# Attention feeding a channel mix: mu spread by one fp32 matmul, wk loaded by whole rows, one load on another queue, new planner settings

## The chip, the cores and the metric

The kernel runs on one core of one Trainium2 chip. The metric is device time in microseconds (us). An execution's profile gives a span from the first to the last instruction; the device time of the same execution is a little longer.

## The reference

```python
q_s = exp(q - max_d(q));  q_s /= sum_d(q_s)        # q, k, v: (8 batches, 8 heads, 576, 64)
k_s = exp(k - max_s(k));  k_s /= sum_s(k_s)
attn = q_s @ (k_s^T @ v)                           # per batch and head
x = attn, heads side by side                       # (8, 576, 512)
x_prev = x shifted by one position, zero first
xk = mu_k * x + (1 - mu_k) * x_prev                # mu_k, mu_r: 512 values
xr = mu_r * x + (1 - mu_r) * x_prev
k = relu(xk @ w_k);  v = (k * k) @ w_v             # w_k 512x1024, w_v 1024x512
out = sigmoid(xr @ w_r) * v                        # w_r 512x512, fp32 out
```

The kernel drops the maxima, since exp of these inputs is small, and works its matmuls in bf16.

## The kernel before

**Tiling.** A batch is done as two groups g = 0, 1 of four heads. Positions are laid as 64 partitions by J = 9, two heads on one partition column block, so that a raw tile (`raw_a` to `raw_l`, twelve buffers) holds q, k or v of one batch and group in fp32: two halves `u`, 288 KB each. Channels of the channel mix are four tiles `ct` of 128; group g makes tiles 2g and 2g+1. F is eight tiles `fc`.

**Attention of one group.** ScalarE: exp of q (`eq`) and k (`ek`), cast of v (`vv`). VectorE: row sums and reciprocals of q (`rsum`, `rrec`, L427 and L430), scaled q (`qs`, L435). TensorE: nine transposes (L462), whose result ScalarE copies to `qt` (L466); the k-v product with a column of ones (L443), whose column sums give `rz` (L450, L454). For batch 0 VectorE multiplies the k-v product with `rz` and with `mu_mask` into `wp` (L503), so that TensorE makes the mixed `xk` and `xr` by itself (L515) and ScalarE or VectorE only copies them out (L520). For batches 1 to 7 TensorE makes x (L556) with weights `w` (L550), ScalarE copies it (`xb`, L561), and VectorE does the rest: an edge copy, the difference `xd` (L569), its scaling by `mu` (`xm`, L574) and the sum `xk` or `xr` (L579).

**mu.** `mu` (one column per mu and channel tile) comes from `mu_sb` by a small TensorE transpose (L324) and a VectorE copy (L327). `mu_rows` holds the 512 values of each mu on every partition, loaded by four broadcast DMAs of 64 partitions x 1 KB (L333). GpSimd builds `mu_mask` from it (L340, L341), four operations for each mu, in the blocks that VectorE has cleared (L305).

**The channel mix** runs in units of 512 columns of `xk`/`xr` (256 for every fifth): k parts (L636, TensorE, 32 matmuls of 128x512), relu on ScalarE (L621), square on VectorE (L625); then for each 128 positions an r part (L667, four matmuls), tanh on ScalarE (L672), two v parts (L677, four matmuls each), the gate on VectorE (L683) and the store from SP (L693). The first two units are "early": for four `fc` at a time they do channel tiles 0 and 1, and then 2 and 3, since group 0 of a batch is mixed before group 1.

**Weights.** `wk`, `wr` and `wv` are cast to bf16 by DMAs from GpSimd's queue. `wk` comes in halves h of 512 columns of F, each half as two DMAs of 64 partitions. A manual dependency holds the first of them until a load of batch 0 (`first[GATE]`) has landed. The loads of batch 1 and later follow on the same queue. [...]

**Order.** Everything is handed to a planner, which simulates five engines with the costs given to `plan.add` and picks, on each engine, the operation with the best pair (start, key); `LOOK` says how much later an operation may start and still count as ready, `key` is a due time passed back along the dependencies (`SPARE` is added at each step, `AHEAD` moves the mixing of batch 0, 1 and later ones forward). `DMA_RATE`, `DMA_LEAD` and `DMA_TAIL` say when a load is believed to land. Engines run their lists strictly in the order so found. `mm` is four PSUM banks, `att` two pairs of banks.

Of the kernel before, what the change touches and what calls it, by code (L numbers as in the profile page):

```python
# [8 lines left out]
ACT = mybir.ActivationFunctionType  # L9
# [3 lines left out]
F32 = mybir.dt.float32  # L13
# [3 lines left out]
START = 0.7  # L17
HOP = 0.05
LATE = 1e6
SPARE = 0.0  # L20
LOOK = {"PE": 0.03, "ACT": 0.3, "DVE": 0.2, "POOL": 0.03, "SP": 0.03}
AHEAD = (0.0, 2.0, 5.0)
MAIN = 18.5
PACE = 1.23
DMA_RATE = 395.0
DMA_LEAD = 1.9
DMA_TAIL = 0.6

PARTS = {1: [slice(0, 2)], 2: [slice(0, 1), slice(1, 2)]}
FIRST = ((0, 0, ("SP", "ACT")), (1, 0, ("SP", "ACT")), (0, 1, ("SP", "SP")),  # L30
         (0, 2, ("SP", "SP")), (1, 1, ("SP", "SP")), (1, 2, ("SP", "SP")))
ORDER = (0, 1, 2)
SOON = {(1, 0, 0): 1.2, (1, 0, 1): 1.4, (1, 0, 2): 1.5}
GATE = 7
FILL = 0
ON_PE = (0,)
CASTS = (("ACT", "ACT"), ("ACT", "ACT"))
# [24 lines left out]
class Plan:  # L62
# [57 lines left out]
    def order(self):  # L120
        self.set_due()
        free = {}
        self.pe_busy = []
        dma_free = 0.0
        waiting = {}
        for op in self.ops:
            waiting.setdefault(op.engine, []).append(op)
        done = []
        left = len(self.ops)
        while left:  # L130
            chosen = None
            for engine, ops in waiting.items():
                now = free.get(engine, START)
                ready = None
                for op in ops:
                    if any(d.end is None for d in op.deps):
                        continue
                    t = max([now] + [d.end + HOP for d in op.deps])
                    ok = True
                    for slot in op.takes:  # L140
                        got = self.slot_time(slot)
                        if got is None:
                            ok = False
                            break
                        t = max(t, got[0] + HOP)
                    if not ok:
                        continue
                    rank = (max(t, now + LOOK[engine]), op.key)
                    if ready is None or rank < ready[0]:
                        ready = (rank, t, op)  # L150
                if ready is not None and (chosen is None or ready[1] < chosen[1]):
                    chosen = ready
            assert chosen is not None, "no operation can start"
            _, t, op = chosen
            for slot in op.takes:
                slot.index = self.slot_time(slot)[1]
                for part in self.pools[slot.pool][slot.index]:
                    self.user[part] = slot
            occ, lat = op.occ, op.lat
            if op.engine == "PE" and not self.warm(t):  # L160
                occ, lat = 2 * occ, occ + lat
            op.start, op.end = t, t + lat
            if op.size:
                dma_free = max(dma_free, t + DMA_LEAD) + op.size / DMA_RATE
                op.end = dma_free + DMA_TAIL
            if op.engine == "PE":
                self.pe_busy.append((t, t + occ))
            free[op.engine] = t + occ
            waiting[op.engine].remove(op)
            done.append(op)  # L170
            left -= 1
        return sorted(done, key=lambda o: o.start)
# [3 lines left out]
def kernel(  # L176
# [12 lines left out]
    nc = tc.nc  # L189

    B, H, S, D = q.shape
    C = H * D
    F = moe_w_k.shape[1]
    assert S == 576 and D == 64 and H == 8, f"{q.shape=}"
    J = S // 64
    CT = C // 128
# [9 lines left out]
    plan = Plan(pools, shared)  # L206

    const = ctx.enter_context(tc.tile_pool(name="const", bufs=1))
# [28 lines left out]
    def bank(slot):  # L237
        return ps[slot.pool][slot.index][:]
# [7 lines left out]
    wk_bf = const.tile([128, CT, F], BF16, name="wk_bf")  # L246
    wv_bf = const.tile([128, FT, C], BF16, name="wv_bf")
    wr_bf = const.tile([128, CT, C], BF16, name="wr_bf")
    mu_sb = const.tile([8, 128], F32, name="mu_sb")
    mu = const.tile([128, 8], F32, name="mu")  # L250
    ident = const.tile([128, 128], BF16, name="ident")
    identf = const.tile([8, 8], F32, name="identf")
    mu_rows = const.tile([128, 2, CT, 64], F32, name="mu_rows")
    mu_mask = const.tile([128, 2, 2, CT, 128], F32, name="mu_mask")
    warm = const.tile([1, 1], F32, name="warm")

# [41 lines left out]

    def emit_consts():
        nc.vector.tensor_copy(out=identf[:], in_=ident[0:8, 0:8])  # L300
        for t in vvs:
            nc.vector.memset(t[:, :, 128:130], 1.0)

# [7 lines left out]
            nc.vector.memset(t[:, :, 0:1], 0.0)  # L311

    zero = plan.add("DVE", 0.1, 0.15, -10, emit_warm_zero)
    plan.add("ACT", 2.0, 2.0, 1.5, emit_warm, [zero])
    mu_load = plan.add("POOL", 1.2, 1.2, -9.2, emit_mu_load, size=8.0)
    identity = plan.add("POOL", 0.6, 0.8, -9.1, emit_identity)
    consts = plan.add("DVE", 0.2, 0.3, -9, emit_consts, [identity])
    late_consts = plan.add("DVE", 0.6, 0.7, LATE, emit_late_consts)
    mask_zeros = plan.add("DVE", 1.8, 1.9, 0, emit_mask_zeros)

    mu_slot = Slot("mm")

    def emit_mu():
        nc.tensor.transpose(out=bank(mu_slot)[:, 0:8], in_=mu_sb[:], identity=identf[:])  # L324
# [1 line left out]
    def emit_mu_copy():  # L326
        nc.vector.tensor_copy(out=mu[:], in_=bank(mu_slot)[:, 0:8])  # L327

    def emit_mu_rows_load(m):
        src = (moe_mu_k, moe_mu_r)[m]  # L330
        for u in range(2):
            ap = bass.AP(tensor=src.tensor, offset=src.offset + 256 * u, ap=[[0, 64], [1, 256]])
            nc.gpsimd.dma_start(  # L333
                out=mu_rows[64 * u:64 * u + 64, m, :, :].rearrange("p c e -> p (c e)"), in_=ap)

    def emit_mu_mask(m):

        for u in range(2):
            r = slice(64 * u, 64 * u + 64)
            nc.gpsimd.tensor_copy(out=mu_mask[r, m, 0, :, r], in_=mu_rows[r, m, :, :])  # L340
            nc.gpsimd.tensor_scalar(out=mu_mask[r, m, 1, :, r], in0=mu_rows[r, m, :, :],  # L341
                                    scalar1=-1.0, scalar2=1.0, op0=ALU.mult, op1=ALU.add)

    mu_t = plan.add("PE", 0.2, 0.4, -500, emit_mu, [mu_load, consts], [mu_slot])
    mu_done = plan.add("DVE", 0.08, 0.17, 0, emit_mu_copy, [mu_t], gives=[mu_slot])
    mu_masked = []
    for m in range(2):
        o = plan.add("POOL", 1.4, 1.4, -9.5 + m, lambda m=m: emit_mu_rows_load(m), size=131.0)
        mu_masked.append(plan.add("POOL", 1.6, 1.7, -2 + m, lambda m=m: emit_mu_mask(m),
                                  [o, mask_zeros]))  # L350

    def filler(slot):
        for _ in range(2):
# [6 lines left out]
                 [slot])  # L360

    def weight_part(dst, src, n, u, c0, c1):
        ap = bass.AP(tensor=src.tensor, offset=src.offset + 4 * u * D * n + c0,
                     ap=[[n, 64], [D * n, CT], [1, c1 - c0]])
        return nc.gpsimd.dma_start(out=dst[64 * u:64 * u + 64, :, c0:c1], in_=ap)

    gate = [first[GATE]]
    sync = mybir.DependencyInfo(mybir.DependencyClass.Sync, mybir.DependencyReason.DATA)

    def emit_wk(h):  # L370
        for u in range(2):
            ld = weight_part(wk_bf, moe_w_k, F, u, 512 * h, 512 * h + 512)
            if h == u == 0:
                tc.add_manual_dep(ld.ins, gate[0].made.ins.name, sync)

    wk_done, wv_done = [], []
    for h in range(2):
        wk_done.append(plan.add(
            "POOL", 1.25, 1.25, h, lambda h=h: emit_wk(h), gate, size=1048.0))
    wr_done = plan.add("POOL", 1.25, 1.25, 2, lambda: [  # L380
        weight_part(wr_bf, moe_w_r, C, u, 0, C) for u in range(2)], gate, size=1048.0)

    def emit_wv(h):
        n = FT // 2
# [4 lines left out]
    for h in range(2):  # L389
        wv_done.append(plan.add("POOL", 0.75, 0.75, 3 + h, lambda h=h: emit_wv(h), gate,  # L390
                                size=1048.0))
# [217 lines left out]
    def unit(half, c0, n):  # L609
# [33 lines left out]
        for f0 in range(0, FT, step):  # L643
            kfs = [Slot("mm") for _ in range(step)]
            mms_ = [None] * step
            for cts in ((0, 1), (2, 3)) if early else (range(CT),):
                gs = sorted({ct // 2 for ct in cts})
                for i in range(step):
                    fc = f0 + i
                    mms_[i] = plan.add(  # L650
                        "PE", per * len(cts), per * len(cts) + 0.17, clock,
                        lambda kf=kfs[i], fc=fc, cts=cts: k_part(kf, fc, cts),
                        [o for b in bs for g in gs for o in mixed[b, g, 0]]
                        + [wk_done[fc // 4], mms_[i]],
                        [kfs[i]] if cts[0] == 0 else [])
                    clock += PACE * per * len(cts)
            for i in range(step):
                kdone.append(mms_[i])
                relu_square(f0 + i, kfs[i], mms_[i])
        rdone = []  # L660
        for m in range(n // 128):
            c = c0 + 128 * m
# [24 lines left out]
            def store(ot=ot, c=c, half=half):  # L687
                for i in range(2):
# [7 lines left out]
            r = plan.add("PE", 0.864, 1.03, clock, r_part,  # L696
                         [o for b in own for g in range(2) for o in mixed[b, g, 1]] + [wr_done],
                         [rps])
            rdone.append(r)
            t = plan.add("ACT", 0.476, 0.6, clock + 1.5, tanh, [r], [th], [rps])  # L700
            clock += PACE * 0.864
            o = plan.add("PE", 0.864, 1.03, clock, lambda v=v_part: v(range(0, 4)),
                         squares[0:4] + wv_done[0:1], [vps])
# [4 lines left out]
            o = plan.add("DVE", 0.593, 0.683, clock + 1.5, gated, [o, t], [ot], [vps, th])  # L708
# [51 lines left out]
```

The softmax here doesn't subtract the row's maximum and nothing guards it: scores larger than these inputs give would overflow.

## Time and profile before

| what | us |
|---|---|
| median of 8 runs | 214.12 (213.27 to 215.41) |
| the profiled execution | 214.17 |
| its span | 212.4 |
| TensorE busy | 190.8 |
| VectorE busy | 163.3 |
| ScalarE busy | 151.9 |
| GpSimd busy | 44.8 |

The profile gives each engine's busy time, the chain of waits that ended last, and the instructions in order of time with the idle time before each and what ended it. Busy time is an average over the span; a stretch of it has to be looked at by itself to see which engine or transfer is late there. For DMAs that cast, the bytes that the profile counts are those written.

### The profile page before, as it was taken

What the parts mean: (1) busy time and instruction counts of PE and PEld (TensorE: products, weight loads), DVE (VectorE), ACT (ScalarE), POOL (GpSimd) and SP (SyncE); (2) the same over time, 40 slices, a digit from 0 to 9 for tenths busy, and PEclk for the clock granted to TensorE, in tenths of its full rate; (3) what the DMA queues carried; (4) which work ended last, traced back from release to release, by engine and by line L of the source; (5) the groups of instructions that cost most, each with busy time, mean ns of one, the idle gap of its engine ahead of it and who ended that gap; (6) DMA issues with size and microseconds to landing.
All of it is one profiled execution on the core that took longest, in us unless ns stands there. A gap on an engine that the chain in (4) does not pass through costs nothing.

```text
span 212.4 us, 3596 instructions
## 1 busy us (share of the span) xinstructions
PE 190.8 (90%) x1281; PEld 97.1 (46%) x1281; DVE 163.3 (77%) x363; ACT 151.9 (72%) x228; POOL 44.8 (21%) x76
## 2 busy tenths in 40 slices
PE   0279698977999999999999999999999999999990
PEld 0254244533544445544466544454544554444740
DVE  4947561999999999999988999698779548942521
ACT  4684696999799999697449997956794665452430
POOL 7385744744433422121000000000000000000000
PEclk9999999999999999999999999999999999999999
DMA  6999999999999999889371040422043022402514
GB/s 217 317 253 204 319 203 378 386 409 404 391 401 400 393 412 403 305 233 302 99 221 39 3 99 0 100 57 47 0 99 90 12 52 49 99 0 49 125 28 99
DMA packets 16530, 40.88 MB, mean 192 GB/s; under 512 B 2360, under 2 KB 4928, under 8 KB 16512
## 3 DMA queue, kind: packets, MB, share of 16 engines
q0 software_dynamic: 9024, 27.66, 40.1%
q1 hardware_dynamic: 7200, 12.39, 20.5%
q10 hardware_dynamic: 288, 0.59, 0.8%
q8 instruction: 10, 0.16, 0.3%
q14 instruction: 8, 0.07, 0.1%
HBM read 33.82 MB, written 9.44 MB: 204 GB/s over the span
## 4 chain that ended last, share of the span: by engine, by line
PE 75%; DMA 12%; DVE 7%; ACT 1%; POOL 1%; SPq 1%; issue 1%; DVEq 0%
PE mm_b L677 9%; PE mm_a L677 7%; PE mm_d L677 7%; PE mm_a L636 6%; PE mm_c L636 6%; PE mm_b L636 6%; PE mm_c L677 5%; PE mm_d L667 5%; PE mm_d L636 5%; DMA wv_bf<-in_moe_w_v_dram 4%; DMA wk_bf<-in_moe_w_k_dram 4%; DMA raw_d<-in_v_dram 4%; PE mm_c L667 4%; PE mm_a L667 3%; PE att_b L443 3%; PE att_a L462 2%
## 5 line engine op out<-in xcount | busy, mean ns | idle before, releaser
L636 PEld LDWEIGHTS <-wk_bf 128*128 128x128 bf16 x320 | 30.6, 98 | 36.0 <-issue 6.5
L636 PE MATMUL mm_c<-xk,wk_bf 128*128 128x512 bf16 (+1 forms) x88 | 21.7, 359 | 4.3 <-DVE xk L579 2.2
L677 PEld LDWEIGHTS <-k_a 128*128 128x128 bf16 x144 | 13.3, 98 | 16.2 <-issue 1.4
L636 PE MATMUL mm_a<-xk,wk_bf 128*128 128x512 bf16 (+1 forms) x84 | 20.5, 359 | 0.1
L667 PEld LDWEIGHTS <-xr 128*128 128x128 bf16 x144 | 13.3, 98 | 15.3
L677 PEld LDWEIGHTS <-k_b 128*128 128x128 bf16 x144 | 13.3, 98 | 15.0
L636 PE MATMUL mm_d<-xk,wk_bf 128*128 128x512 bf16 (+1 forms) x72 | 18.0, 361 | 0.0
L636 PE MATMUL mm_b<-xk,wk_bf 128*128 128x512 bf16 (+1 forms) x76 | 17.7, 351 | 0.0
L677 PE MATMUL mm_b<-wv_bf,k_a 128*128 128x512 bf16 x56 | 14.4, 379 | 0.0
L462 PE MATMUL att_a<-ident,qs_a 128*128 128x128 bf16 x72 | 5.8, 231 | 8.2 <-DVE qs_a L435 8.2
L667 PE MATMUL mm_d<-wr_bf,xr 128*128 128x512 bf16 x48 | 12.3, 380 | 0.0
L677 PE MATMUL mm_a<-wv_bf,k_b 128*128 128x512 bf16 x48 | 12.3, 379 | 0.0
L677 PE MATMUL mm_d<-wv_bf,k_a 128*128 128x512 bf16 x40 | 10.3, 379 | 1.1 <-DMA wv_bf<-in_moe_w_v_dram 1.1
L667 PE MATMUL mm_c<-wr_bf,xr 128*128 128x512 bf16 x40 | 10.3, 379 | 0.0
L677 PE MATMUL mm_b<-wv_bf,k_b 128*128 128x512 bf16 x40 | 10.1, 379 | 0.0
L462 PEld LDWEIGHTS <-qs_a 128*128 128x128 bf16 x72 | 5.0, 103 | 9.8 <-DVE qs_a L435 8.4
L667 PE MATMUL mm_a<-wr_bf,xr 128*128 128x512 bf16 x36 | 9.2, 379 | 0.0
L672 ACT ACTIVATE th_a<-mm_c 128x512 f32<-128x512 f32 x9 | 5.5, 614 | 4.7 <-PE mm_c L667 3.0
L677 PE MATMUL mm_c<-wv_bf,k_b 128*128 128x512 bf16 x32 | 8.2, 379 | 0.0
L621 ACT ACTIVATE rel_c<-mm_c 128x512 bf16<-128x512 f32 (+1 forms) x11 | 6.2, 562 | 2.5 <-PE mm_c L636 2.2
L672 ACT ACTIVATE th_b<-mm_a 128x512 f32<-128x512 f32 x8 | 4.8, 602 | 4.4 <-PE mm_a L667 4.3
L466 ACT COPY qt_a<-att_a 128x1152 bf16<-128x1152 bf16 x5 | 5.6, 1118 | 2.9 <-PE att_a L462 2.9
(250 smaller groups left out, 450.7 us busy)
## 6 DMA issues: line engine op xcount, KB each, us to landing
out_dram<-ot_a SPq DMA_DIRECT2D x24, 128.0 KB, 2.4
out_dram<-ot_b SPq DMA_DIRECT2D x24, 128.0 KB, 2.6
out_dram<-ot_c SPq DMA_DIRECT2D x24, 128.0 KB, 2.8
raw_a<-in_q_dram POOLq DMA_DIRECT2D x3, 576.0 KB, 11.6
raw_b<-in_k_dram POOLq DMA_DIRECT2D x3, 576.0 KB, 12.2
raw_f<-in_v_dram POOLq DMA_DIRECT2D x3, 576.0 KB, 11.0
raw_g<-in_q_dram POOLq DMA_DIRECT2D x3, 576.0 KB, 12.1
raw_e<-in_k_dram POOLq DMA_DIRECT2D x2, 576.0 KB, 11.2
```

The lines of the kernel that those rows point to most:

```text
L443: nc.tensor.matmul(kv_of(kvp, hf)[:, 0:129], lhsT=eks[ek.index][r, j, :, :].rearrange("p u d -> p (u d)"), rhs=vvs[vv.index][r, j, 0:129], ...
L462: nc.tensor.transpose(out=transposed()[:, j, :], in_=qss[qs.index][:, j, :], identity=ident[:])
L466: nc.scalar.copy(out=qts[qt.index][:], in_=transposed()[:, 0:J, :])
L621: nc.scalar.activation(out=rels[rel.index][:, 0:n], in_=bank(kf)[:, 0:n], func=ACT.Relu, scale=HALF_ROOT)
L636: nc.tensor.matmul(bank(kf)[:, 0:n], lhsT=wk_bf[:, ct, fc * 128:(fc + 1) * 128], rhs=xs[0][:, ct, c0:c0 + n], start=(ct == 0), stop=(ct == ...
L667: nc.tensor.matmul(bank(rps), lhsT=xs[1][:, ct, c:c + 128], rhs=wr_bf[:, ct, :], start=(ct == 0), stop=(ct == CT - 1))
L672: nc.scalar.activation(out=ths[th.index][:], in_=bank(rps), func=ACT.Tanh, scale=0.5)
L677: nc.tensor.matmul(bank(vps), lhsT=k2s[k2.index][:, ft, 128 * m:128 * m + 128], rhs=wv_bf[:, ft, :], start=(ft == 0), stop=(ft == FT - 1))
```

## The change

- Loads of mu: `mu_rows` becomes two partitions of 2 x 256 values, loaded by two small DMAs. One fp32 matmul with a 2 x 128 selector (`pick`, made by VectorE from `ident`) writes them to all 128 partitions of a PSUM bank, ScalarE copies them to `mu_wide`, and GpSimd's four operations for each half of `mu_mask` read that.
- `wk` is loaded in halves of two channel tiles with all 1024 columns (4 KB of a row of HBM for each piece) where it was all four tiles with 512 columns. A k part now depends on the halves that hold its tiles.
- The second half of batch 0's k of group 0 is issued from ScalarE's queue, not SP's. The gate of the weight loads is the first half of group 0's v, not the second.
- Of batch 1, q and k of both groups are asked for around `wr`, and v after `wv`; before, all of group 0 came ahead of `wr`, and group 1 after `wv`.
- Settings of the planner, and small loads no longer queue behind large ones in its model.

```diff
-SPARE = 0.0
-LOOK = {"PE": 0.03, "ACT": 0.3, "DVE": 0.2, "POOL": 0.03, "SP": 0.03}
-AHEAD = (0.0, 2.0, 5.0)
+SPARE = 0.2
+LOOK = {"PE": 0.1, "ACT": 0.5, "DVE": 0.3, "POOL": 0.03, "SP": 0.03}
+AHEAD = (2.0, 6, 2)
 MAIN = 18.5
-PACE = 1.23
-DMA_RATE = 395.0
-DMA_LEAD = 1.9
+PACE = 1.183
+DMA_RATE = 365.0
+DMA_LEAD = 2.5
-FIRST = ((0, 0, ("SP", "ACT")), (1, 0, ("SP", "ACT")), (0, 1, ("SP", "SP")),
+FIRST = ((0, 0, ("SP", "ACT")), (1, 0, ("SP", "ACT")), (0, 1, ("SP", "ACT")),
...
-SOON = {(1, 0, 0): 1.2, (1, 0, 1): 1.4, (1, 0, 2): 1.5}
-GATE = 7
+SOON = {(1, 0, 0): 1.2, (1, 1, 0): 1.5, (1, 0, 1): 2.5, (1, 1, 1): 2.7}
+GATE = 6
...
-            if op.size:
+            if op.size and op.size < 20:
+                op.end = t + lat + 2.2
+            elif op.size:
...
-    mu_rows = const.tile([128, 2, CT, 64], F32, name="mu_rows")
+    mu_rows = const.tile([2, 2, 256], F32, name="mu_rows")
+    mu_wide = const.tile([128, 2, CT, 64], F32, name="mu_wide")
+    pick = const.tile([2, 2, 64], F32, name="pick")
...
+        nc.vector.tensor_copy(out=pick[:], in_=ident[0:2, 0:2, None].to_broadcast((2, 2, 64)))
...
-    plan.add("ACT", 2.0, 2.0, 1.5, emit_warm, [zero])
+    plan.add("ACT", 1.6, 1.7, 3.5, emit_warm, [zero])
...
-    def emit_mu_rows_load(m):
-        src = (moe_mu_k, moe_mu_r)[m]
-        for u in range(2):
-            ap = bass.AP(tensor=src.tensor, offset=src.offset + 256 * u, ap=[[0, 64], [1, 256]])
-            nc.gpsimd.dma_start(
-                out=mu_rows[64 * u:64 * u + 64, m, :, :].rearrange("p c e -> p (c e)"), in_=ap)
+    def emit_mu_rows_load():
+        for m, src in enumerate((moe_mu_k, moe_mu_r)):
+            nc.gpsimd.dma_start(out=mu_rows[:, m, :], in_=bass.AP(
+                tensor=src.tensor, offset=src.offset, ap=[[256, 2], [1, 256]]))
+
+    def emit_mu_rows():
+        nc.tensor.matmul(bank(rows_slot), lhsT=pick[:].rearrange("p u c -> p (u c)"),
+                         rhs=mu_rows[:].rearrange("p m c -> p (m c)"), start=True, stop=True)
+
+    def emit_mu_wide():
+        nc.scalar.copy(out=mu_wide[:].rearrange("p m c e -> p (m c e)"), in_=bank(rows_slot))
...
-    mu_masked = []
-    for m in range(2):
-        o = plan.add("POOL", 1.4, 1.4, -9.5 + m, lambda m=m: emit_mu_rows_load(m), size=131.0)
-        mu_masked.append(plan.add("POOL", 1.6, 1.7, -2 + m, lambda m=m: emit_mu_mask(m),
-                                  [o, mask_zeros]))
+    rows_load = plan.add("POOL", 1.3, 1.3, -600, emit_mu_rows_load, size=10.0)
+    rows_done = plan.add("PE", 0.86, 0.98, -501, emit_mu_rows, [rows_load, consts], [rows_slot])
+    wide = plan.add("ACT", 0.48, 0.6, 0, emit_mu_wide, [rows_done], [], [rows_slot])
+    mu_masked = [plan.add("POOL", 1.55, 1.6, -2 + m, lambda m=m: emit_mu_mask(m),
+                          [wide, mask_zeros]) for m in range(2)]
...
-        ap = bass.AP(tensor=src.tensor, offset=src.offset + 4 * u * D * n + c0,
-                     ap=[[n, 64], [D * n, CT], [1, c1 - c0]])
-        return nc.gpsimd.dma_start(out=dst[64 * u:64 * u + 64, :, c0:c1], in_=ap)
+        ap = bass.AP(tensor=src.tensor, offset=src.offset + (4 * u + c0) * D * n,
+                     ap=[[n, 64], [D * n, c1 - c0], [1, n]])
+        return nc.gpsimd.dma_start(out=dst[64 * u:64 * u + 64, c0:c1, :], in_=ap)
...
-            ld = weight_part(wk_bf, moe_w_k, F, u, 512 * h, 512 * h + 512)
+            ld = weight_part(wk_bf, moe_w_k, F, u, 2 * h, 2 * h + 2)
...
-                        + [wk_done[fc // 4], mms_[i]],
+                        + [wk_done[ct // 2] for ct in cts[::2]] + [mms_[i]],
```

More of the change, by code (lines that the diff above doesn't have):

```diff
@@ L319 @@
     mask_zeros = plan.add("DVE", 1.8, 1.9, 0, emit_mask_zeros)
-    mu_slot = Slot("mm")
+    mu_slot, rows_slot = Slot("mm"), Slot("mm")
     def emit_mu():
@@ L339, in emit_mu_mask @@
             r = slice(64 * u, 64 * u + 64)
-            nc.gpsimd.tensor_copy(out=mu_mask[r, m, 0, :, r], in_=mu_rows[r, m, :, :])
-            nc.gpsimd.tensor_scalar(out=mu_mask[r, m, 1, :, r], in0=mu_rows[r, m, :, :],
+            nc.gpsimd.tensor_copy(out=mu_mask[r, m, 0, :, r], in_=mu_wide[r, m, :, :])
+            nc.gpsimd.tensor_scalar(out=mu_mask[r, m, 1, :, r], in0=mu_wide[r, m, :, :],
                                     scalar1=-1.0, scalar2=1.0, op0=ALU.mult, op1=ALU.add)
@@ L380 @@
     wr_done = plan.add("POOL", 1.25, 1.25, 2, lambda: [
-        weight_part(wr_bf, moe_w_r, C, u, 0, C) for u in range(2)], gate, size=1048.0)
+        weight_part(wr_bf, moe_w_r, C, u, 0, CT) for u in range(2)], gate, size=1048.0)
     def emit_wv(h):
```

## The prediction

> **What bounds the kernel now.** First the busy times by engine and the bars over 40 slices: TensorE is busy for 190.8 of 212.4 us, at full granted clock, and its row is full from about 60 us on.
>
> ```profile
> PE   0279698977999999999999999999999999999990
> DVE  4947561999999999999988999698779548942521
> DMA  6999999999999999889371040422043022402514
> ```
>
> So an edit can only be worth something in the first 60 us, or by making TensorE late after that. The windows add up its idle time from its first k part (19.2 us): 1.17 us in 20–24, 0.84 in 24–28, 0.51 in 28–32, 0.60 in 32–36, 2.63 in 44–60, together **5.75 us**, and none in 60–200. VectorE has 48.56 of 50 us in 60–110: it keeps up, with little to spare.
>
> Second, the chain of waits up to 49 us, in order of time (start, length, what):
>
> ```profile
> 3.34 7.79 DMA raw_d<-in_v_dram
> ...
> 11.42 1.90 POOL wk_bf L365 x3
> 13.32 8.86 DMA wk_bf<-in_moe_w_k_dram
> ...
> 22.46 0.63 POOL wr_bf L365
> 23.16 9.39 DMA wv_bf<-in_moe_w_v_dram
> 32.59 1.02 PE mm_d L677 x4
> ...
> 48.00 0.76 DVE xk L579
> ```
>
> The reader should see a DMA queue: v of batch 0, wk, then wv, until 32.6 us; then TensorE, until it waits for batch 1's xk at 48.8. Third, the timelines by engine, for the gaps themselves (idle before and releaser in brackets):
>
> ```profile
> 24.84 0.59 PE L636 MATMUL mm_c<-xk,wk_bf 128*128 128x512 bf16 x2 [2.01 <-ACT rel_a L621]
> 32.59 1.02 PE L677 MATMUL mm_d<-wv_bf,k_a 128*128 128x512 bf16 x4 [1.11 <-DMA wv_bf<-in_moe_w_v_dram]
> 48.82 0.59 PE L636 MATMUL mm_c<-xk,wk_bf 128*128 128x512 bf16 x2 [2.22 <-DVE xk L579]
> 22.90 1.41 ACT L413 ACTIVATE eq_c<-raw_g 128x576 bf16<-128x576 f32 x2 [2.84 <-DMA raw_g<-in_q_dram]
> 36.02 0.17 DVE L450 RECIPROCAL rz_c<-att_b 128x2 f32<-128x2 f32 x1 [4.02 <-PE att_b L443]
> 7.74 0.61 POOL L340 COPY mu_mask<-mu_rows 64x256 f32<-64x256 f32 x1 [2.79 <-DMA mu_rows<-in_moe_mu_k_dram]
> 11.42 2.54 POOL L365 DMA_DIRECT2D wk_bf<-in_moe_w_k_dram  x4 [1.86 <-DMA raw_d<-in_v_dram]
> ```
>
> The first gap is a relu queued behind an exp whose q had not landed; the second is wv; the third is batch 1's mixing. VectorE idles 4 us until 36.0 and then does the sums and scaling of group 1's q (37.66–40.6) just when batch 1 is due.
>
> Fourth, DMA by window (last two columns: busy share of the engines, GB/s written):
>
> ```profile
> 14.00:16.00 2.00, 1.89 (x23) 1.33 (x22) 1.27 (x5) 2.00 (x4) 1.93 (x5) 1.00 1.05 158
> 16.00:18.00 2.00, 1.77 (x18) 0.84 (x14) 1.89 (x9) 0.79 (x2) 2.00 (x5) 1.00 0.96 130
> 28.00:30.00 2.00, 2.00 (x19) 1.04 (x17) 0.72 (x2) 2.00 (x5) 1.08 (x2) 1.00 1.24 205
> ```
>
> The engines are full throughout. Weights are read as fp32 and written as bf16, so reads are twice these figures: 316 and 260 GB/s while wk comes in, 410 while wr and wv do.
>
> [...] SP's issue of that slot takes 0.4–0.6 us, the landing 6 to 9. [...] here five matmuls of L515 take 1.17 us at 13.9 and 0.66 from 17.1.
>
> **The change, part by part.**
>
> *mu.* Removed: 4 x 64 KB of broadcast, 0.26 MB, 0.75 us of DMA at about 350 GB/s (4–8 us: 339). Added: two small DMAs (1.2 us of issue, the first things on GpSimd's queue), the fp32 matmul, a ScalarE copy (0.6 us, as the 128x512 tanh), a tiny VectorE copy. A bf16 matmul of 512 columns takes 0.216 us in a warm stream (0.864 for four)[...]. No trace row shows how fast such small loads land first in the queue. Bounds: from issue to landing, 2.8 us net of data in the idle machine (raw loads late in the kernel: 4.2 for 576 KB, which take 1.4) and 6.4 (`mu_sb`, behind the broadcasts). I take 4.4: the second lands at 1.35 + 4.4 = 5.7, the matmul ends at 7.6, `mu_wide` at 8.2. ScalarE waits meanwhile, with the exps of `eq_b` (5.73 to 6.98) behind it; then 1.25 + 1.36 + 0.67 us of work bring it to about 11.5 before the last cast of `raw_d`, which ended at 11.83. VectorE's `mu` copy may come ahead of `qs_a` and wait to about 8; VectorE idled for 1.98 us before 13.05, which covers that. Nothing on the path there. Without this slack, 1 us each.
>
> *GpSimd behind it.* Both mask halves (1.8 + 1.6 us) now probably stand ahead of wk: 8.2 + 3.4 = 11.6. Before, half the masks did, and wk began at 11.42. So the earlier gate (raw_d's first half landed by 9.55) gains nothing, and DMA engines that finish batch 0 0.75 us sooner wait for wk: **+0.2 us** for wk, and the mu bytes save nothing. In return the 0.73 us VectorE wait for the second mask half goes, off the path.
>
> *wk by rows.* The same bytes in pieces twice as long. 2.1 MB at 290 GB/s (the mean of 316 and 260) is 7.2 us, at 410 it is 5.1. Bounds 0 and −2.1; a loss is as little likely as a shorter row being faster. I take **−1.5** for all that lands after.
>
> *The moved slot.* ScalarE issues a third DMA (0.45 us): its table load goes to 2.1, the warm exp ends at 3.6, before `raw_a` lands at 4.38. SP issues `raw_d` 0.5 us sooner; in a full DMA that is hidden. Nothing.
>
> *Batch 1.* Ahead of wv there are now four loads of 0.59 MB, not three: +0.59 MB at 408 GB/s = +1.45. wv: 32.55 + 0.2 − 1.5 + 1.45 = **32.7**, unchanged. wr, with one load less before it: 30.1 + 0.2 − 1.5 − 1.45 = 27.4. v of group 1, last of batch 1: 38.8 + 0.2 − 1.5 = 37.5.
>
> *TensorE to wv.* Idle between the first k part and wv is 2.01 + 1.11 and some small. q arrives 1.3 sooner, so the relu stall shrinks to about 0.7, and with wr there at 27.4 two of the three r parts that ran after wv (33.45, 37.64, 39.86) fit before it: 2 x 0.864 = −1.7. It would reach batch 1's xk at 46.6 − 1.7 = 44.9.
>
> *Batch 1's xk.* It now takes from 38.87 (cast of v) to 48.76. With q and k done in VectorE's 4 us gap, the chain is cast 1.43, k-v 0.65, rz and w 0.8, x 0.5, copies 1.1, edge and difference 0.95, scaling 0.9, sum 0.76 = 7.1, and 1.5 of queueing: 37.5 + 8.6 = 46.1, **2.7 sooner**. TensorE waits 1.2 us there, and goes on at 46.1 instead of 48.8. This last gap sets the sum, so the terms before it are not added.
>
> *Planner.* TensorE's LOOK of 0.1 may leave up to 0.07 us more before each of 56 attention pieces: between 0 and 3.9 us; its lists have been backlogged (no idle in 60–200), so I take +0.1. VectorE must follow 2.7 us sooner: batch 2's xk ended at 69.38 for a k part at 70.72. The 3.2 us of q work moved ahead of 36 us pay for it.
>
> **Sum:** −2.7 + 0.1 = −2.6. The profiled execution took 214.17 (span 212.4), so 211.6, span 209.8; its time is the median's within 0.05, so 211.5.
>
> **Rivals.**
>
> - *Late rows (slower).* The small loads land as late as `mu_sb` did, at 9.67. Then matmul 11.5, `mu_wide` 12.2, masks 15.6, wk issued 4.2 us later than before, with the DMA engines dry from 13. Against the central case that is +4.0: 215.5. It decides above a landing of 5.7 + 2.6 = 8.3 us. For it: every small load so far took about 6 us. Against it: those came behind 64 KB pieces; these are first.
> - *Worse order.* AHEAD from 5 to 2 for later batches lets VectorE take other work first; slack before units 3 and 4 was 1.34 and 1.07 us (the latter 90.20 to 91.27). One late xk of 2 to 3 us in two units eats the gain: 214 to 216.
> - *wk by rows is worth nothing.* All of batch 1 comes 1.5 later: 213.0.
> - *All idle goes.* Of 5.75 us, 1 stays: 209.4.
>
> **How the numbers follow.** Central 0.42 (210.5 to 212.7), wk without gain 0.18, all idle gone 0.14, late rows 0.14, worse order 0.12 (half of it near no change). Faster by over 0.3% (0.64 us, about what a measurement of this kernel can tell from no change): 0.73; same 0.08; slower 0.19. Range 209.2 to 215.0; about one in ten lies above.
>
> **What would show it.** Right: `mu_wide` read on GpSimd near 8 us; wk issued near 11.6 and all landed by 21; TensorE waiting for wv near 32.7 with r parts before it; the xk wait near 46; no idle after 60. Wrong: wk issued after 13, GB/s below 150 while it loads, or TensorE gaps after 60 us released by VectorE's xk.

## The result, and the profile after

| | before | after |
|---|---|---|
| median | 214.2 (31 runs) | 216.74 (11 runs, 215.47 to 218.21) |
| profiled execution, span | 214.17, 212.4 | 216.56, 214.8 |
| TensorE busy, and idle in the span | 190.8, 21.6 | 192.0, 22.8 |
| VectorE, ScalarE, GpSimd busy | 163.3, 151.9, 44.8 | 163.6, 153.5, 45.8 |

Runs of both on one chip give a ratio of 1.0109 [1.0083, 1.0134]: the change is **slower by 1.1%** (2.5 us by the medians), above the predicted range, and went the way of the late-rows rival.

The bars of the changed kernel, each digit 5.4 us, the busy share in tenths, with the bytes written:

```profile
PE   0358866996999999999999999999999999999990
DVE  4399287279999999999957995998699958952431
DMA  6918999999999996997572380314042122402424
GB/s 207 394 60 133 290 258 231 394 399 406 393 392 406 405 390 218 292 280 269 138 249 53 102 305 4 71 31 98 0 101 60 39 48 53 92 6 49 102 49 98
```

TensorE's row is full to the end from about the same place as before; the damage is in the first five slices. The third slice of DMA, a 9 before, is now a 1. The windows show how empty it is (length, busy time with counts of PE, PE's weight loads, VectorE, ScalarE, GpSimd, then TensorE's granted clock, busy share of the DMA engines, GB/s). The first three lines are the changed kernel's, the last is the kernel before:

```profile
12.00:14.00 2.00, 1.14 (x9) 0.98 (x10) 2.00 (x6) 2.00 (x4) 1.88 (x5) 1.00 0.00 0
14.00:16.00 2.00, 1.82 (x26) 1.62 (x26) 1.72 (x6) 2.00 (x4) 1.96 (x4) 1.00 0.00 0
16.00:18.00 2.00, 1.89 (x20) 1.33 (x20) 1.87 (x7) 2.00 (x4) 2.00 (x4) 1.00 0.35 44
...
12.00:14.00 2.00, 2.00 (x28) 1.80 (x26) 0.83 (x5) 2.00 (x4) 1.96 (x4) 1.00 0.94 243
```

From 12 to 16 us all 16 DMA engines do nothing, where before they wrote 243 and 158 GB/s in the same two windows. The chain of waits (start, length, what) says why:

```profile
1.95 5.94 DMA mu_rows<-in_moe_mu_r_dram
...
8.03 2.04 PE mm_a L340 x2
...
10.12 0.58 ACT mu_wide L344
...
10.76 0.71 POOL mu_mask L350
11.47 0.89 POOL mu_mask L351
...
15.82 0.61 POOL wk_bf L375
...
17.59 7.23 DMA wk_bf<-in_moe_w_k_dram
...
25.11 8.53 DMA raw_i<-in_k_dram
```

Where the chain before began with the loads of batch 0, it now begins with 2 KB of mu. The timelines (idle before and releaser in brackets) show who else stood still for it:

```profile
8.03 2.04 PE L340 MATMUL mm_a<-mu_rows,pick 2*128 2x512 f32 x2 [8.03 <-DMA mu_rows<-in_moe_mu_r_dram]
10.11 0.59 ACT L344 COPY mu_wide<-mm_a 128x512 f32<-128x512 f32 x1 [4.22 <-PE mm_b L329]
10.14 0.17 DVE L332 COPY mu<-mm_b 128x8 f32<-128x8 f32 x1 [3.38 <-PE mm_b L329]
10.76 0.71 POOL L350 COPY mu_mask<-mu_wide 64x256 f32<-64x256 f32 x1 [6.44 <-ACT mu_wide L344]
15.77 2.44 POOL L375 DMA_DIRECT2D wk_bf<-in_moe_w_k_dram  x4
22.08 0.59 PE L646 MATMUL mm_c<-xk,wk_bf 128*128 128x512 bf16 x2 [1.13 <-DMA wk_bf<-in_moe_w_k_dram]
49.88 0.59 PE L646 MATMUL mm_c<-xk,wk_bf 128*128 128x512 bf16 x2 [1.01 <-DVE xk L589]
```

All four compute engines wait for loads that their lists place first: ScalarE with `eq_b` behind `mu_wide` (exp at 10.59, before at 5.73), VectorE with the scaling of q behind the copy of `mu`, TensorE with the transposes behind the matmul, GpSimd with the masks and `wk` behind them. `wk` is issued at 15.77, 4.35 us later than before; the first k part starts at 22.08, not 19.21 (+2.9). From there to 60 us TensorE idles 5.4 us (37.92 less 32.49 busy; before 5.75). So 2.9 − 0.3 = 2.6 us are lost ahead of the k parts and hardly any is won back later; the spans differ by 2.4.

### The profile page after: what moved, and what is told of

Its sections match the earlier page's. It is cut to its first block, busy times and chain, and to the rows that moved or that the text cites. A ratio compares the mean times of both kernels' runs of the same rounds, so it can differ in the third digit from the quotient of the medians.

```text
span 214.8 us, 3600 instructions
## 1 busy us (share of the span) xinstructions
PE 192.0 (89%) x1283; PEld 97.5 (45%) x1283; DVE 163.6 (76%) x364; ACT 153.5 (71%) x229; POOL 45.8 (21%) x74
## 4 chain that ended last, share of the span: by engine, by line
PE 78%; DMA 10%; DVE 4%; POOL 3%; issue 1%; ACT 1%; DVEq 0%; ACTq 0%; POOLq 0%
PE mm_c L646 8%; PE mm_a L687 7%; PE mm_d L687 7%; PE mm_b L687 7%; PE mm_d L646 7%; PE mm_c L687 7%; PE mm_a L646 6%; PE mm_b L646 5%; PE mm_a L677 4%; DMA raw_i<-in_k_dram 4%; PE mm_d L677 4%; DMA wk_bf<-in_moe_w_k_dram 3%; PE mm_c L677 3%; PE mm_b L677 3%; DMA mu_rows<-in_moe_mu_r_dram 3%; PE att_b L453 2%
## 5 line engine op out<-in xcount | busy, mean ns | idle before, releaser
L646 PE MATMUL mm_c<-xk,wk_bf 128*128 128x512 bf16 (+1 forms) x100 | 23.8, 353 | 4.4 <-DVE xk L589 1.8
L646 PE MATMUL mm_d<-xk,wk_bf 128*128 128x512 bf16 (+1 forms) x84 | 20.7, 359 | 0.0
L646 PE MATMUL mm_a<-xk,wk_bf 128*128 128x512 bf16 (+1 forms) x72 | 18.3, 367 | 0.0
L646 PE MATMUL mm_b<-xk,wk_bf 128*128 128x512 bf16 (+1 forms) x64 | 15.1, 353 | 0.0
L687 PE MATMUL mm_d<-wv_bf,k_b 128*128 128x512 bf16 x40 | 10.3, 379 | 0.0
L682 ACT ACTIVATE th_a<-mm_a 128x512 f32<-128x512 f32 x10 | 6.0, 604 | 4.7 <-PE mm_a L677 3.5
L677 PE MATMUL mm_d<-wr_bf,xr 128*128 128x512 bf16 x36 | 9.2, 379 | 0.0
L687 PE MATMUL mm_c<-wv_bf,k_a 128*128 128x512 bf16 x32 | 8.2, 379 | 0.0
L677 PE MATMUL mm_b<-wr_bf,xr 128*128 128x512 bf16 x32 | 8.2, 379 | 0.0
L687 PE MATMUL mm_a<-wv_bf,k_a 128*128 128x512 bf16 x32 | 8.2, 379 | 0.0
```

Of the source, the lines that this page charges most:

```text
L646: nc.tensor.matmul(bank(kf)[:, 0:n], lhsT=wk_bf[:, ct, fc * 128:(fc + 1) * 128], rhs=xs[0][:, ct, c0:c0 + n], start=(ct == 0), stop=(ct == ...
L677: nc.tensor.matmul(bank(rps), lhsT=xs[1][:, ct, c:c + 128], rhs=wr_bf[:, ct, :], start=(ct == 0), stop=(ct == CT - 1))
L682: nc.scalar.activation(out=ths[th.index][:], in_=bank(rps), func=ACT.Tanh, scale=0.5)
L687: nc.tensor.matmul(bank(vps), lhsT=k2s[k2.index][:, ft, 128 * m:128 * m + 128], rhs=wv_bf[:, ft, :], start=(ft == 0), stop=(ft == FT - 1))
```

## The experiments

The first theory: the order of the lists comes from the planner's belief that a small load lands 2.2 us after its issue. In the changed kernel the small loads land after 5.2 to 5.9 us. The engines are held for what the planner thought had come; everything else in the change is worth about what the prediction says. Rival: the `wk` queue alone is at fault, as the late-rows rival has it. All ratios below are to the kernel before, run on the same chip; differences between experiments are taken from the ratios, times 214.2 us. "The wait for `xk`" is TensorE's longest idle time for batch 1.

**e1: the right belief.** One number of the changed kernel:

```diff
-                op.end = t + lat + 2.2
+                op.end = t + lat + 5.9
```

> The changed kernel, in whose planner small loads are believed to land 5.9 us after their issue (measured: 5.9 for the second mu_rows load), not 2.2. The planner then puts wk's first half ahead of the masks on GpSimd's queue, and the exps of eq_b and ek_a ahead of mu_wide on ScalarE. Theory (wk stands behind masks that wait for the rows): wk's first load is issued near 10 instead of 15.8, no dry DMA stretch of 5 us, 211.0 to 213.5 us. Rival A (waits of ScalarE, VectorE and TensorE on the rows are what costs): the same gain, since those go too. Rival B (wk by rows, the order of batch 1 or the planner's settings cost by themselves): 216 or more.

Measured: **212.23** us, 0.991 [0.988, 0.9941], span 210.1. The matmul of the rows still has to wait for them to 7.7, but nothing else is held up for long. GpSimd now issues the first half of `wk`, then builds the masks, then issues the second half; from its and TensorE's timelines:

```profile
9.37 1.21 POOL L375 DMA_DIRECT2D wk_bf<-in_moe_w_k_dram  x2 [5.05 <-DMA raw_d<-in_v_dram]
14.17 1.25 POOL L375 DMA_DIRECT2D wk_bf<-in_moe_w_k_dram  x2
45.79 0.59 PE L646 MATMUL mm_c<-xk,wk_bf 128*128 128x512 bf16 x2 [1.12 <-DVE xk L589]
```

So 4.3 us of the changed kernel's time (1.0109 less 0.991) hang on the order of its lists, and the kernel with that number mended beats the one before by 0.9%. That is a gain of 1.9 us where the prediction had 2.6, with the wait for `xk` ending near the forecast place (45.8, forecast 46.1).

**e2: wk ahead of the masks, the rest left waiting.** The masks get a dependency on the gate in the plan, and `wk` an early key:

```diff
-                          [wide, mask_zeros]) for m in range(2)]
+                          [wide, mask_zeros, first[GATE]]) for m in range(2)]
-            "POOL", 1.25, 1.25, h, lambda h=h: emit_wk(h), gate, size=1048.0))
+            "POOL", 1.25, 1.25, -700 + h, lambda h=h: emit_wk(h), gate, size=1048.0))
```

> The changed kernel with all four wk loads ahead of the masks on GpSimd's queue; ScalarE, VectorE and TensorE still wait for the rows as before the edit. Theory: wk issued near 10, landed near 19; TensorE's wait for batch 1's xk ends near 47 instead of 52; 211.5 to 213.5 us. Rival A: eq_b still starts near 10.6 and the first k-v product near 14.2, so 215.5 to 217. Rival B: 216 or more.

Measured: 215.22, 1.0047 [1.0024, 1.0071]. `wk` is issued at 8.86, yet 2.9 us of the 4.3 stay lost. GpSimd's and ScalarE's timelines:

```profile
8.86 2.37 POOL L375 DMA_DIRECT2D wk_bf<-in_moe_w_k_dram  x4 [4.56 <-DMA raw_d<-in_v_dram]
10.39 1.26 ACT L423 ACTIVATE eq_b<-raw_b 128x576 bf16<-128x576 f32 x2
```

`eq_b` still runs only at 10.4, and the chain of waits goes through the rows, `mu_wide` and ScalarE's line instead of through the masks. So `wk` is not the only thing held up: the rival of one queue falls. Not all of the 2.9 is the wait itself: in the profiled execution the wait for `xk` ends 1.8 us after e1's (47.63 against 45.79), it is 2.98 us long, and the granted clock is 0.59 from 48 to 52 us (see the last section).

**e7: e2 with the right belief.**

> e1 with both halves of wk ahead of the masks. In e1 the DMA engines run nearly dry in 14 to 16 us (26 GB/s), since the second half waits for the masks. If the DMA stream still sets the end: wv and batch 1 land 1 to 1.5 us sooner, 210.8 to 211.7 us. If TensorE now needs the masks (1.3 us later here) more: 212.3 to 213.5.

Measured: 212.24, 0.9928 [0.9899, 0.9957], the same as e1. No DMA engine is dry now, but nothing more is won. In the profiled execution TensorE waits 2.83 us for `xk`, to 45.75, and its clock then falls to 0.56 (see the last section).

**e13: e1 with wk behind the masks.** The mirror of e2: only GpSimd's order for batch 0 is undone.

```diff
-    gate = [first[GATE]]
+    gate = [first[GATE]] + mu_masked
```

> The kernel of e1, with one thing undone: wk stands behind all eight mask operations on GpSimd, as in the change, while ScalarE, VectorE and TensorE keep e1's order for batch 0 and wait for no small load. Masks from 10.4 to about 13.9, wk issued at 13.9 (e1: 9.4 and 14.2 for its halves), the DMA engines dry for some 2 us before. If wk's lateness is a chain of its own, as the prediction's late-rows rival had it: first k part near 20.5, batch 1 some 2 us later than in e1, the xk wait ends near 48, 214 to 215. If it only matters together with the other engines' waits: 212.2 as e1.

Measured: **219.17**, 1.0225 [1.0188, 1.0262], 4 to 5 us slower than expected. `wk` is issued at 14.59, after `mu_wide` at 10.77, and its windows show the hole again:

```profile
12.00:14.00 2.00, 2.00 (x27) 1.80 (x27) 0.73 (x4) 2.00 (x4) 1.84 (x6) 1.00 0.03 10
14.00:16.00 2.00, 1.08 (x10) 0.60 (x9) 1.75 (x6) 2.00 (x4) 2.00 (x5) 1.00 0.00 0
```

The wait for `xk` ends at 49.02, 3.2 us later than in e1. The rest is later still: TensorE idles another 0.7, 1.4 and 1.2 us in 49–52, 52–56 and 60–80 us, where e1 idles 0.2 at most. The planner, told of the late `wk`, also orders the later batches otherwise; which of these stops belongs to `wk` and which to the new order was not taken apart. Nor is it known how much of the 3.2 us is the new order's. What e2 and e13 show together is that neither half of the mending is enough by itself (+2.9 and +6.7 against e1), and that the two losses don't add up to the 4.3 of the changed kernel.

**e11 and e14: which small load.** The late belief for the rows alone, and for `mu_sb` alone (the rows have size 10, `mu_sb` size 8):

```diff
-                op.end = t + lat + 2.2
+                op.end = t + lat + (5.9 if op.size > 9 else 2.2)     # e11
+                op.end = t + lat + (2.2 if op.size > 9 else 5.9)     # e14
```

> The change, with the late belief (5.9 us) for the rows of mu alone; the loads of mu_sb stay believed to land 2.2 us after issue. GpSimd's and ScalarE's lists are those of e1; only VectorE's copy of mu and TensorE's small transpose come ahead of q's scaling again, as in the change, and wait for mu_sb to 10 us. If the wait of GpSimd and ScalarE for the rows is the whole loss: 212.2, as e1. If VectorE's wait for mu_sb is a chain of its own: first transposes near 11.9, as in the change without the matmul, and 213.5 to 214.5.

> The change, with the late belief (5.9 us) for the loads of mu_sb alone. GpSimd's and ScalarE's lists are exactly the change's: masks ahead of wk, mu_wide ahead of eq_b; only VectorE's copy of mu and TensorE's transpose of mu_sb go behind the scaling of q, so VectorE does not stop until 10 us. If ScalarE and GpSimd, waiting for the rows, are the cause: 215.5 to 216.7, near the change. If VectorE's stop was the larger part: 214 or less.

Measured: e11 215.33, 1.0042 [1.002, 1.0063]; e14 215.99, 1.0076 [1.0045, 1.0107]. Neither mends much. In e14, VectorE no longer stops for `mu`, but ScalarE and TensorE do for the rows (`vv_a` is the last of the operations queued behind `mu_wide`):

```profile
10.02 0.59 ACT L344 COPY mu_wide<-mm_a 128x512 f32<-128x512 f32 x1 [4.16 <-PE mm_a L340]
14.09 0.27 PE L453 MATMUL mm_c<-vv_a,ek_a 64*128 64x129 bf16 x1 [2.83 <-ACT vv_a L430]
```

e11 is less clean than planned. TensorE's list has the transpose of `mu_sb` ahead of the row matmul, so the rows came late after all: `mu_sb` landed at 9.27, the matmul ran at 9.38, and ScalarE waited 1.71 us for it. It shows that a wait for `mu_sb` on TensorE and VectorE costs about as much as one for the rows, not that VectorE alone does.

**e8 and e12: the small loads on SP's queue.** e8 moves all four to SP behind `raw_a`'s half, with the belief left; e12 adds the edit of e2 and a belief of 3.9 us, the landing seen in e8.

```diff
-            nc.gpsimd.dma_start(out=mu_rows[:, m, :], in_=bass.AP(
+            nc.sync.dma_start(out=mu_rows[:, m, :], in_=bass.AP(
-    rows_load = plan.add("POOL", 1.3, 1.3, -600, emit_mu_rows_load, size=10.0)
+    rows_load = plan.add("SP", 0.9, 0.9, 0.5, emit_mu_rows_load, size=10.0)
...
```

> The changed kernel with mu_rows and mu_sb loaded from SP's queue, behind raw_a's first half, and the planner's belief of 2.2 us left as it is. If 5.9 us is what GpSimd's queue takes at the start: landing 2 to 4 us after issue, mu_wide near 7.5, wk issued near 11, 212 to 213.5 us. If it is the full DMA engines that hold small loads up: landing 5 to 6 us after issue as before, wk near 15 and 215.5 to 217.5 us.

> The small loads on SP's queue behind raw_a's first half, believed to land 3.9 us after issue as they did there, and wk held ahead of the masks on GpSimd. Rows at 5.7, mu_wide at 7.8 behind exps that are ready, masks from about 9 to 13 us beside the landing wk. If both of the change's waits (GpSimd's and the other engines') are all that was lost: 211.5 to 212.5, as e1 or a little better. If SP's eight outstanding loads (raw_b issued at 4.9) cost: first kv near 12.5 and 213 to 214.

Measured: e8 214.69, 1.004 [1.0012, 1.0068]; e12 214.78, 1.0015 [0.9994, 1.0037]. In e8 the second load of the rows lands 3.94 us after its issue, at 5.5, but the masks end only at 13.5 and `wk` is still 2.1 us late. In e12 the matmul of the rows starts at 5.05 and no engine waits for them for long, and it is still 2.2 us short of e1. SP's and GpSimd's timelines suggest why:

```profile
2.14 0.30 SPq L291 DMA_DIRECT2D mu_sb<-in_moe_mu_r_dram  x1
4.73 0.36 SPq L275 DMA_DIRECT2D raw_b<-in_q_dram  x1
10.11 2.54 POOL L375 DMA_DIRECT2D wk_bf<-in_moe_w_k_dram  x4 [8.80 <-DMA raw_d<-in_v_dram]
```

Once SP has issued five loads and ScalarE three, SP issues nothing from 2.44 to 4.73, with eight of batch 0's twelve halves still to go. The gate (the first half of `raw_d`) opens at 10.1. That this is what costs the 2.2 us is not shown: the gate opens at 10.2 in e7's profiled execution too, and between 8.9 and 9.9 in e1, e2, e6, e9 and e10, whose loads of batch 0 go out alike. TensorE waits 1.86 us for `vv_a` at 11.33 and, at the end of the line, 2.96 us for `xk` at 47.73.

**e15: the rows first of all.** Only the two row loads go to SP, ahead of `raw_a`; `mu_sb` stays on GpSimd with the late belief.

```diff
-            nc.gpsimd.dma_start(out=mu_rows[:, m, :], in_=bass.AP(
+            nc.sync.dma_start(out=mu_rows[:, m, :], in_=bass.AP(
-    rows_load = plan.add("POOL", 1.3, 1.3, -600, emit_mu_rows_load, size=10.0)
+    rows_load = plan.add("SP", 0.7, 0.7, -600, emit_mu_rows_load, size=10.0)
-                op.end = t + lat + 2.2
+                op.end = t + lat + (2.2 if op.size > 9 else 5.9)
```

> The two loads of the rows are the first of all, on SP's queue ahead of raw_a (issued near 0.7 and 1.0), believed to land 2.2 us after issue; mu_sb stays on GpSimd with the late belief. If what stands ahead of a load decides: the rows land by about 3.5, the matmul ends near 5.6, masks run from about 6.5 to 10, wk is issued near 10 with nothing held up: 211 to 212.5, e1 or better; raw_a some 0.5 us later. If a small load takes 5 to 6 us whatever stands ahead: rows at 6.5, ScalarE idle 2 us with half of eq_a and all of eq_b behind, wk near 12.5, 214 to 215.5. If the two more loads among SP's outstanding ones decide (raw_d later, as in e12): 213.5 to 215 with the rows early.

Measured: **212.08**, 0.9902 [0.987, 0.9934], level with e1. TensorE's and GpSimd's timelines:

```profile
3.57 2.04 PE L340 MATMUL mm_a<-mu_rows,pick 2*128 2x512 f32 x2 [3.57 <-DMA mu_rows<-in_moe_mu_r_dram]
6.30 0.39 POOL L350 COPY mu_mask<-mu_wide 64x256 f32<-64x256 f32 x1 [3.39 <-ACT mu_wide L344]
10.02 2.45 POOL L375 DMA_DIRECT2D wk_bf<-in_moe_w_k_dram  x4
```

Issued at 0.75 and 1.18, the rows are there by 3.57. Now the order that the change was built on (matmul, masks, then `wk`) works: the masks fill GpSimd's idle time before `wk`'s gate. So the loss goes away in two ways, by planning for the late landing (e1) and by making the landing early (e15).

From issue to landing the second load of the rows takes 2.3 us here, with one half of batch 0 issued ahead of it, about 3.4 and 3.9 with three (e12, e8), and 5.9 with six (the changed kernel). The DMA issues (engine, count, KB each, us to landing) show what the large loads take, first in the changed kernel, then in e8, then in e15:

```profile
raw_c<-in_k_dram SPq DMA_DIRECT2D x1, 288.0 KB, 6.3
raw_c<-in_k_dram ACTq DMA_DIRECT2D x1, 288.0 KB, 6.5
mu_rows<-in_moe_mu_k_dram POOLq DMA_DIRECT2D x1, 2.0 KB, 5.2
mu_rows<-in_moe_mu_r_dram POOLq DMA_DIRECT2D x1, 2.0 KB, 5.9
...
raw_c<-in_k_dram ACTq DMA_DIRECT2D x1, 288.0 KB, 4.6
...
raw_c<-in_k_dram ACTq DMA_DIRECT2D x1, 288.0 KB, 6.4
mu_sb<-in_moe_mu_k_dram POOLq DMA_DIRECT2D x1, 2.0 KB, 5.4
```

In the changed kernel 2 KB issued at 1.95 land at 7.9, with the 288 KB of `raw_c` issued at 1.65 (8.0): its size did not help it. But what stands ahead does not decide alone. ScalarE's half of `raw_c` goes out at the same time (1.67 and 1.65) behind the same three halves in e8 and e15; it takes 4.6 us in e8, where SP issues nothing large until 4.92, and 6.4 in e15, where SP issues two more halves at 1.86 and 2.33. And `mu_sb` in e15, issued by GpSimd at 1.57 behind three halves, still takes 5.4 us. So the loads issued just after count too, or GpSimd's queue adds 1.5 to 2 us of its own (5.4 against 3.4 and 3.9 from SP); no run here gives GpSimd a small load with little around it, and the two stay unseparated.

**e3, e4, e5: the mu part by itself.** e3 is the changed kernel with the four broadcasts back; e5 is e3 with the late belief (which there touches `mu_sb` alone); e4 is the kernel before with the mu part alone, `wk` in column halves.

```diff
-    mu_rows = const.tile([2, 2, 256], F32, name="mu_rows")
-    rows_done = plan.add("PE", 0.86, 0.98, -501, emit_mu_rows, [rows_load, consts], [rows_slot])
...
+    mu_rows = const.tile([128, 2, CT, 64], F32, name="mu_rows")
+        o = plan.add("POOL", 1.4, 1.4, -9.5 + m, lambda m=m: emit_mu_rows_load(m), size=131.0)
...
```

> The changed kernel with only the mu part undone: mu_rows by four broadcast DMAs, no fp32 matmul. Theory: wk issued near 11.5, everything else of the change keeps its worth: 211.5 to 213.5 us. Rival A: the same. Rival B: 216 or more.

> The kernel before with only the mu part of the change. Theory: masks near 10.8 to 15.8, wk issued near 15.8, 4.4 us later than before, and nothing to set against it: 217 to 219 us. Rival A: 216 to 217 (the first k-v product 2.3 us later). Rival B: 213.5 to 214.8.

> mu_rows by broadcast as in e3, and small loads believed to land after 5.9 us, so that VectorE's mu copy comes late in its list instead of behind the first row sums. If the 3 us by which e3 missed e1 are VectorE's and TensorE's wait for mu_sb, this gives 211.5 to 213 us (first transposes near 8.2). If the broadcast itself costs them (0.26 MB more, masks in another place), it stays at 214.5 to 215.5.

Measured: e3 215.17, 1.0039 [1.0017, 1.0062]; e4 **220.04**, 1.0265 [1.022, 1.031]; e5 213.06, 0.9949 [0.992, 0.9978]. Under the wrong belief the matmul costs 1.5 us against the broadcast (1.0109 and 1.0039) and 5.7 us in the kernel before, where `wk` goes out at 14.23 instead of 11.42. Under the right one it is about 0.8 us better (e1 and e5, intervals that overlap). e3 loses 1.9 us to `mu_sb` alone: VectorE waits for it to 10.12 with q's scaling behind.

**e6: e1 with wk in column halves.** `weight_part`, its calls and the k part's dependency as before.

> e1 with wk in halves of 512 columns of all four channel tiles again. If whole rows are worth the 1.5 us of the prediction: 213.2 to 214.2 us and lower GB/s while wk is loaded. If rows only change the piece size and nothing waits for it: 211.8 to 212.7.

Measured: 213.29, 0.9966 [0.9953, 0.998]. By these ratios whole rows and the dependency that goes with them are worth about **1.2 us** (e1 0.991). The traces don't show the transfer itself to be so much faster. Of the 1.2 us between the two profiled executions, 0.9 is there at the first k part (17.29 and 16.37), which waits for no `wk` in either; in e6 the second half of `raw_c` was late, before `wk` was issued at all. And where the DMA engines had run dry before it, `wk` took 8.9 to 9.05 us from first issue to last landing by rows (the changed kernel, e13, e14) and 9.5 by columns (e4).

**e9 and e10: batch 1's order and the planner's settings**, each put back in e1.

```diff
-SOON = {(1, 0, 0): 1.2, (1, 1, 0): 1.5, (1, 0, 1): 2.5, (1, 1, 1): 2.7}      # e9
+SOON = {(1, 0, 0): 1.2, (1, 0, 1): 1.4, (1, 0, 2): 1.5}
-LOOK = {"PE": 0.1, "ACT": 0.5, "DVE": 0.3, "POOL": 0.03, "SP": 0.03}         # e10, with
+LOOK = {"PE": 0.03, "ACT": 0.3, "DVE": 0.2, "POOL": 0.03, "SP": 0.03}        # SPARE, AHEAD, PACE, DMA_*
```

> The kernel of e1 (the change, with small loads believed to land 5.9 us after issue), but batch 1's loads in the old order: all of group 0 ahead of wr, group 1 after wv. If the prediction's step for batch 1 was right (q and k of both groups ahead of wv bring v of group 1 and so the last xk sooner), group 1's q, k and v now come after wv, its row sums and scaling fall into the time in which VectorE mixes group 0, and the xk wait ends near 48 rather than 45.8: 213.6 to 214.5. If the order is worth nothing once wk is by rows: 212.2 as e1, xk wait near 46.

> The kernel of e1 with the planner's settings of before (SPARE, LOOK, AHEAD, PACE, and rate and lead of loads). The prediction gave the settings +0.1 us with 0 to 3.9 open: 212.1 if that holds. If the new LOOK of TensorE cost something in 56 pieces, this is faster, 209 to 211.5; if the new settings are what lets VectorE keep the batches in time, slower, 213 to 215, with waits of TensorE for xk after 60 us. With these settings the list has wk wholly ahead of the masks, so GpSimd's order differs too.

Measured: e9 214.3, 0.9999 [0.9977, 1.0021]; e10 212.26, 0.9902 [0.9867, 0.9937]. The new order of batch 1 is worth **1.9 us**, and its wait ends 2.6 us later without it, as TensorE's timeline of e9 shows; 1.0 of the 2.6 is there at the first k part of that execution (17.33 against 16.37), which the order of batch 1 can't explain. The settings are worth nothing that can be measured.

```profile
48.35 0.59 PE L646 MATMUL mm_c<-xk,wk_bf 128*128 128x512 bf16 x2 [2.86 <-DVE xk L589]
```

The parts put back one by one (0.8 for the matmul against the broadcast, 1.2, 1.9) add up to 3.9 us, and e1 gains 1.9: they overlap, or the moved slot and the earlier gate, which no run puts back by themselves, cost something.

## Why the prediction was wrong

**The step that failed** is "I take 4.4: the second lands at 1.35 + 4.4 = 5.7, the matmul ends at 7.6, `mu_wide` at 8.2". GpSimd issues the second load at 1.95 and it lands 5.9 us later, at 7.9 (0.6 us of the lateness is the issue, 1.5 the landing); the matmul ends at 10.1 and `mu_wide` at 10.7. The bounds (2.8 to 6.4) held; the choice between them rested on "these are first". They are the first on GpSimd's queue only: at 1.95, SP and ScalarE had issued six halves of 288 KB, and the second load came in with the last of these. The issue times were in the trace of before, where SP's loads go out at 0.75, 1.20 and 1.66, and so was the busy share of the DMA engines, 1.02 from 4 to 8 us. The full engines were reckoned with for the moved slot ("in a full DMA that is hidden") and not for the small loads. (The landing of that slot, read as "6 to 9", is 6.0 and 6.6 us for the two halves in the trace of before.)

**"Masks 3.4 us"** was the second mis-sized term: they took 5.05 (10.76 to 15.8). Eight operations at the durations before would have ended at 14.2 and `wk` with them. The timelines of GpSimd and VectorE in the changed kernel show what ran beside them:

```profile
11.47 0.88 POOL L351 TENSOR_SCALAR mu_mask<-mu_wide 64x256 f32<-64x256 f32 x1
12.77 0.41 POOL L351 TENSOR_SCALAR mu_mask<-mu_wide 64x256 f32<-64x256 f32 x1
13.60 0.99 POOL L351 TENSOR_SCALAR mu_mask<-mu_wide 64x256 f32<-64x256 f32 x1
10.47 1.62 DVE L445 TENSOR_TENSOR qs_a<-eq_a,rrec_a 128x576 bf16<-128x576 bf16 x2
12.01 1.40 DVE L437 TENSOR_REDUCE rsum_b<-eq_b 128x9 f32<-128x576 bf16 x2
13.58 1.61 DVE L445 TENSOR_TENSOR qs_b<-eq_b,rrec_b 128x576 bf16<-128x576 bf16 x2
```

The same operation takes 0.88 and 0.99 us beside VectorE's multiplication of q, and 0.41 beside its row sum. The multiplication is slower too: 1.62 for the two halves, 1.42 in the kernel before. Why the two are slower together is not shown. The late rows had put the masks beside that multiplication.

**"+0.2 us" for wk** became +4.35 with these two terms. **"Nothing on the path there"** for ScalarE and VectorE was wrong too. The stated slack was 0.3 us on ScalarE (11.5 against 11.83) and 1.98 on VectorE; ScalarE's `eq_b` moved by 4.9. The cover was real only for the central landing, and the text said "1 us each" without it; in e2 the waits of ScalarE, VectorE and TensorE together cost 2.9.

**The late-rows rival** had the mechanism, the hole in the DMA and nearly the amount: 215.5 predicted, 216.74 measured, `wk` 4.2 us late against 4.35. The nearness of these two is in part luck: the rows landed at 7.9 and not at the rival's 9.67, and masks of 5.05 us instead of 3.4 made up for most of it. Its price was worked for GpSimd alone, and its threshold of 8.3 us was too high: with masks of 5 us a landing at 7.9 was enough. It was given 0.14, because every small load before had followed 64 KB pieces; that GpSimd's small loads take 5 to 6 us among the loads of batch 0 (5.2 to 5.9 in the changed kernel, 5.4 for `mu_sb` in e15) was the better reading.

**What was right.** The fp32 matmul: 1.9 us by the prediction's times (5.7 to 7.6), 2.04 measured, in two records. The 1.9 was the author's estimate; what makes the matmul so much longer than the 0.216 us of a bf16 one of 512 columns is not shown. Batch 1's xk "2.7 us sooner": 3.0 in e1 (45.79, before 48.82), with its order of loads worth 1.9. The planner +0.1: 0, give or take 1. `wk` by rows −1.5: −1.2 as a number, but it stood for a faster transfer, and that was shorter by only about 0.5 us where the traces can be compared (9.0 against 9.5). And the sum, once nothing is held up: 211.5 against 212.23 in e1 and 212.08 in e15. This too is by another way than forecast: in neither does TensorE wait for wv (the first v part runs at 31.4 and 32.3; forecast was a wait to 32.7), and in e1 half of `wk` goes ahead of the masks. TensorE's idle time after the first k part in e1 is 3.98 us where it was 5.75. The sign that was to show failure came: `wk` issued after 13 and no DMA while it should load.

## What to carry to other kernels

In a list that is worked strictly in order, a believed landing time is a wait: one constant that was 3.7 us too small cost 4.3 us, more than the change could win, since four engines stood behind it. So before small loads are put on the path of the start, look up what is issued around them on every queue, and either issue them first of all (2.3 us here, from SP) or plan for the landing of the big load issued beside them (5.9). And cost a wait for every engine that has the waiting instruction in its list, not for the one with the longest story.

## What was not expected of the hardware

- **After waits of 2.83 to 2.98 us TensorE's granted clock was 0.56 to 0.65.** In 17 traces there are four such stops between 40 and 64 us, of 2.83 (e7), 2.86 (e9), 2.96 (e12) and 2.98 us (e2), and each is followed by such a clock in the window of 48–52 us. Of three stops of 2.0 to 2.2 us, one is followed by such a dip (e4, 2.02) and two are not (before, 2.22; e13, 2.23), and none of the shorter ones is. The window of e12 and a pair of k-part matmuls of e7:

```profile
48.00:52.00 4.00, 4.00 (x12) 1.41 (x11) 3.93 (x10) 3.53 (x5) 1.55 (x3) 0.57 1.04 406
```

```profile
46.56 1.06 PE L646 MATMUL mm_d<-xk,wk_bf 128*128 128x512 bf16 x2
```

At a granted clock of 1.00 such a pair shows as 0.59 (before, 48.82). In e7 seven pairs start 0.84 us apart (45.75 to 51.61), where 0.43 is usual: 2.9 us, as much again as the wait. What lowers the clock is not shown. The dip does not come in every execution: three of e7's fifteen have a mean granted clock of 1.00 (211.55 to 212.0 us), the others 0.983 to 0.989 (211.77 to 214.53 us). So the 2.9 us are not always lost in the end.

- **SP stopped after four loads of 2 KB and four of 288 KB as it did after eight of 288 KB.** In e12 four small loads and four halves of batch 0 have gone out from SP's and ScalarE's queues when SP stops issuing, from 2.44 to 4.73 us. In the changed kernel the eight are all halves, and SP stops from 3.33 to 4.82, until the first half of `raw_a` lands. Whether the chip or the program makes SP stop is not shown.
